# Moving two blocks of work in a routed-attention and feed-forward kernel: pair 0's sums and clusters past the first weight chunk, the last pair's denominators up to its products with v

## The chip, the cores and the metric

The kernel runs on one core of a Trainium2 chip. The metric is the device time of one execution in microseconds (us), lower is better. All times "at 18.26" are counted from the start of the span of the profiled execution. The engines are TensorE (PE in the profile; PEld is its weight load), VectorE (DVE), ScalarE (ACT), GpSimd (POOL) and SyncE (SP), which issues most of the DMA transfers. Each engine works through its own instructions in order; an instruction that waits holds up what stands behind it on the same engine.

## The reference

Four batches, eight heads, 768 tokens, 64 values per head, 16 clusters per head. A query sees only the keys of its own cluster. The result, with the heads side by side, goes through a normalisation and a two-layer feed-forward block (512 to 2048 to 512).

```python
q_n = q / (norm(q) + 1e-6); k_n = ...; c_n = ...
q_assign = argmax(q_n @ c_n.T, axis=-1)
k_assign = argmax(k_n @ c_n.T, axis=-1)
mask = q_assign[:, None] == k_assign[None, :]
scores = where(mask, q @ k.T / sqrt(D), -1e9)
attn = exp(scores - max) ; attn = attn / (sum(attn) + 1e-9)
x = attn @ v                      # heads side by side: (4, 768, 512)
xn = (x - mean) / sqrt(var + 1e-6) * g_ln
out = x + maximum(xn @ w_ch1, 0) @ w_ch2
```

The two weight matrices come as 64-bit floats; the kernel turns them into 32-bit floats itself.

## The kernel before, in words

**Attention.** Two heads of a batch make a pair; there are 16 pairs, n = 0 to 15. Each pair has two slots, one for each half of the queries (384), and each slot has six steps, one for each tile of 128 keys. Per step, `scores` multiplies the mask's one-hot rows (a large negative number is added where the clusters differ), then k and q (L385), into a PSUM tile `s_ps`, of which there are three, and ScalarE takes the exponential into `e` (L380). `weigh` multiplies six steps' `e` with v (L397) into `a_ps`, which ScalarE copies to `x` (L412). `add_up` adds the slot's `e` tiles on VectorE (`two`, L432 and L435; for the last pair `es`, L422, five additions).

**Clusters.** For the next pair, VectorE transposes k and q (L282), TensorE multiplies them with the normalised centroids (`sim_ps`, L304), and `prep_route` finds the best cluster on VectorE: transpose, maximum, comparison, transpose (L317, L320, L323, L333), which leaves `oh`. ScalarE makes the mask's rows out of `oh` in `prep_mask` (L350), six pieces in the slot before the pair starts.

**Denominators.** `finish(n, 0)` sums the added-up exponentials over the keys with a matmul by ones (`den_ps`, L451), copies the result on ScalarE (L460), and sends it through DRAM with two POOL transfers (`flat`, `rdens`). `finish(n, 1)` takes the reciprocal on VectorE (L467) and spreads it; parts 2 and 3 multiply `x` by it and store it. For n < 15 `den_ps` is in the pool of `a_ps`; for n = 15 it is a tile of the pool that `ps()` names at that moment.

**Weight chunks.** The weights come in 32 chunks of 512 KB. SP loads a chunk into `raw` (two buffers, L241). `split_weight` takes the words apart on VectorE (L250, L253, L256), `join_weight` builds the 32-bit value from them (L265, L269, L270) and sends the low part as a POOL transfer that adds into `w` (L273). `convert` gives chunk m a place: chunks 0 to 13 go with both slots of pairs 0 to 6, chunks 14 to 21 with the first slot of pairs 7 to 14, the last ten follow in the feed-forward part. `load_weight(m + 2)` stands behind `join_weight(m)`.

**Order.** In the attention part the order of TensorE, VectorE, ScalarE and POOL is the order of the calls in the loop over `u` (pair and slot); SP's transfers are placed by the framework's scheduler there, in an order near to that of the calls. In each slot: scores; the similarities or the masks of the next pair; `split_weight`; `weigh`; `add_up`; `join_weight`; in slot 0 the load of the next pair's v and `prep_route(n + 1)`.

**Hand-over.** After the last pair all pools of the attention part, PSUM's three among them, are closed (`stage.close()`), and a pool of eight PSUM tiles, `ps_m`, takes their place. The feed-forward part begins with the products `x_ps`, `y_ps`, `z_ps` (`first_layer`, L781), copies on ScalarE (`p`, `u`, L796) and additions on VectorE (L801). The last pair's `finish(15, 0)` stands between the second and the third of these products, so its `den_ps` is a tile of `ps_m`. The first blocks of the feed-forward part read batch 0, whose attention is long done.

Of the kernel before, what the change touches and what calls it, by code (L numbers as in the profile page):

```python
# [19 lines left out]
def kernel(  # L20
# [49 lines left out]
    def ps(name, dt=F32, n=512):  # L70
        return pools["t"].tile([P, n], dt, tag="t", name=name)

    pairs = [(b, pr) for b in range(B) for pr in range(NPAIR)]
# [170 lines left out]
    def split_weight(m):  # L244
        words = raws[m].bitcast(U32).rearrange("p (n w) -> p n w", w=2)
        hi = words[:, :, 1]
        ta = pools["conv"].tile([P, WC], U32, tag="ta", name="ta")
        tb = pools["conv"].tile([P, WC], U32, tag="tb", name="tb", bufs=2)

        nc.vector.tensor_scalar(  # L250
            ta, hi, 0x07FFFFFF, 3, op0=ALU.bitwise_and, op1=ALU.logical_shift_left
        )
        nc.vector.scalar_tensor_tensor(  # L253
            out=ta, in0=hi, scalar=0xC0000000, in1=ta, op0=ALU.bitwise_and, op1=ALU.bitwise_or
        )
        nc.vector.tensor_single_scalar(tb, hi, 0x7FF00000, op=ALU.bitwise_and)  # L256
        halves[m] = (ta, tb)
# [56 lines left out]
    def prep_route(n):  # L314

        sim = route.tile([P, HC], F32, tag="sim", name="sim_sb")
        nc.vector.transpose(sim, prepared[n]["sim"][:, :HC])  # L317
        sims = sim.rearrange("p (g c) -> p g c", c=NCL)
        best = route.tile([P, NG], F32, tag="best", name="best")
        nc.vector.tensor_reduce(best, sims, AX.X, ALU.max)  # L320

        onehot = route.tile([P, HC], BF16, tag="onehot", name="onehot")
        nc.vector.scalar_tensor_tensor(  # L323
            out=onehot.rearrange("p (g c) -> p g c", c=NCL),
            in0=sims,
            scalar=1.0,
            in1=best.unsqueeze(2).to_broadcast([P, NG, NCL]),
            op0=ALU.mult,
            op1=ALU.is_equal,
            accum_out=hits[:, n : n + 1],  # L330
        )
        oh = route.tile([P, HC], BF16, tag="oh", name="oh")
        nc.vector.transpose(oh, onehot)  # L333
        prepared[n]["oh"] = oh
# [107 lines left out]
    def finish(n, part):  # L442
        b, pr = pairs[n]
        if part == 0:
            den = ps_a.tile([P, 512], F32, tag="a", name="den_ps") if n + 1 < len(pairs) else ps("den_ps")
            parts = len(sums[n, 0])
            for h in range(parts):
                for j in range(2):
                    for g in range(NHALF):
                        r = (j * NHALF + g) * Q  # L450
                        nc.tensor.matmul(  # L451
                            den[r : r + Q, :HC], ones, sums[n, g][h][:, j, :],
                            start=h == 0, stop=h == parts - 1, tile_position=(0, r),
                            skip_group_check=True,
                        )
            if n + 1 < len(pairs):
                dsb = last.tile([P, HC], F32, tag="dsb", name="dsb", bufs=1)
            else:
                dsb = late["all"][:, 1, :HC]
            nc.scalar.copy(dsb, den[:, :HC])  # L460
            flat = dram.tile([P // Q, HC], F32, tag="flat", name="flat")
            nc.gpsimd.dma_start(out=flat, in_=dsb[0:P:Q, :])
            nc.gpsimd.dma_start(
                out=rdens[:, n, :], in_=flat.rearrange("i (p e) -> (i p) e", e=DE)
            )
        elif part == 1:
            nc.vector.reciprocal(rdens[:, n, :], rdens[:, n, :])  # L467
            row = dram.tile([2, S], F32, tag="row", name="row")
            nc.gpsimd.dma_start(
                out=row.rearrange("j (p e) -> (j p) e", e=DE), in_=rdens[:, n, :]  # L470
            )
            if n + 1 < len(pairs):
                rb = last.tile([P, S], F32, tag="rb", name="rb", bufs=1)
            else:
                rb = late["all"][:, 2]
            for j in range(2):
                nc.gpsimd.dma_start(
                    out=rb[j * D : (j + 1) * D, :],
                    in_=row[j : j + 1, :].to_broadcast([D, S]),
                )  # L480
            late[n] = rb
        elif part == 2:
            a, x = xs.pop(n), late[n]
            if b:
                nc.vector.tensor_tensor(x, a, x, ALU.mult)
                nc.sync.dma_start(out=xT_d[b][pr], in_=x)
            else:
                late[n] = norm_tiles(b)[0][:, pr, :]
                nc.vector.tensor_tensor(late[n], a, x, ALU.mult)
        else:  # L490
            x = late.pop(n)

            if n + 1 < len(pairs):
                y = last.tile([P, S], F32, tag="y", name="y")
            else:
                y = late["all"][:, 0]
            nc.vector.transpose(y, x)
            for i in range(P // Q):
                m = pr * P + i * Q
                nc.sync.dma_start(  # L500
                    out=x_d[b].rearrange("t (a r) m -> r (t a) m", r=Q)[:, :, m : m + Q],
                    in_=y[i * Q : (i + 1) * Q].rearrange("r (g f) -> r g f", f=Q),
                )
# [182 lines left out]
    with tc.manual_schedule(engines=order | {mybir.EngineType.Pool}):  # L686
        for u in range(len(pairs) * slots):
            n, slot = divmod(u, slots)
            nxt = n + 1 < len(pairs)
            own = range(GROUP * u, GROUP * (u + 1))  # L690
            if slot == 0 and not nxt:
                finish(n - 1, 0)
            if slot == 0 and nxt:
                for side in (1, 0):
                    prep_transpose(n + 1, side)
                    load(n + 2, "qk"[side])
            for i in own:
                if i >= AHEAD:
                    scores(i)
            if slot == 0:  # L700
                if n and nxt:
                    finish(n - 1, 0)
                if n:
                    prep_mask(n, *pieces[-1])
                if nxt:
                    prep_sims(n + 1)
            elif nxt:
                for piece in pieces[:-1]:
                    prep_mask(n + 1, *piece)
            for job in extra.pop((n, f"between {slot}"), ()):  # L710
                job()
            if slot and n > 1 and nxt:
                finish(n - 2, 2)
                finish(n - 2, 3)
            m = convert.get((n, slot))
            if m is not None:
                split_weight(m)
            for i in own:
                weigh(i)
            add_up(n, slot, (0,))  # L720
            if slot and n and nxt:
                finish(n - 1, 1)
            if nxt:
                add_up(n, slot, (1,))
            if m is not None:
                join_weight(m)
                load_weight(m + 2)
            if slot == 0:
                load(n + 1, "v")
                if nxt:  # L730
                    prep_route(n + 1)
                else:
                    for part in (2, 3):
                        finish(n - 2, part)
                    finish(n - 1, 1)
            elif not nxt:
                for part in (2, 3):
                    finish(n - 1, part)
            for job in extra.pop((n, slot), ()):
                job()  # L740

# [203 lines left out]
    with tc.manual_schedule(engines=order):  # L945
        first_layer(0, 0, 1)
        first_layer(0, 0, 2)
        finish(len(pairs) - 1, 0)
        first_layer(0, 0, 6)
        w1_sums(0, 0, (2, 3))  # L950
        x_sum(0, 3)
        first_layer(0, 0, 5)
        first_layer(0, 0, 7)
        x_sum(0, 4)
        w1_sums(0, 1)
        for j in range(1, NFH):
            first_units(0, j)
            if j in (1, 3):
                for part in ((1,), (2, 3))[j // 2]:
                    finish(len(pairs) - 1, part)  # L960
# [252 lines left out]
```

## Time and profile before

| | |
|---|---|
| median of 5 runs | 919.44 us (918.18, 919.24, 919.44, 920.58, 921.9) |
| profiled execution | 917.51 us, span 915.5 us |
| granted TensorE clock | 0.998 |
| TensorE matmuls | 905.1 us busy, 99% of the span |
| VectorE | 605.8 us, 66% |
| ScalarE | 365.3 us, 40% |
| GpSimd | 78.1 us, 9% |
| DMA | 89.33 MB, mean 98 GB/s |

The page gives each engine's busy time, then forty slices of the span with the busy share in tenths. Rows of groups and of the timeline name the source line, the engine, the operation and the tiles it writes and reads (`e<-s_ps`); `[0.61 <-DVE oh L333]` behind a row of the timeline says that the engine stood idle for 0.61 us before it and that VectorE's `oh` ended the wait. In the table of waits the columns are total, times and the longest. Attention lasts from about 9 to 329 us, the feed-forward part from there to the end. From 20 to 310 us VectorE is busy about nine tenths of the time as well.

### The profile page before, as it was taken

The page shows a single profiled execution, that of the slowest core. Times are in us where ns is not written, and L with a number is a line of the kernel's source. Part 1 is how long each engine was busy: PE and PEld are TensorE (multiplying, and loading weights), DVE is VectorE, ACT ScalarE, POOL GpSimd, SP SyncE. Part 2 cuts the span into 40 slices and gives each one's busy share as a digit, 9 for nine tenths or more (in the row PEclk, how much of TensorE's full clock was granted, in tenths as well). Part 3 has the DMA queues.
Part 4 walks back from the last instruction along what each step waited for, and adds up shares of the span by engine and source line. Part 5 has one row for each costly group of instructions (what it writes and reads, how often), then busy time and mean ns, then how long its engine had stood idle before and what let it go on. Part 6 is the DMA issues. An engine that isn't in the chain of part 4 may idle for free.

```text
span 915.5 us, 12230 instructions
## 1 busy us (share of the span) xinstructions
PE 905.1 (99%) x4556; PEld 577.1 (63%) x4556; DVE 605.8 (66%) x1060; ACT 365.3 (40%) x619; POOL 78.1 (9%) x141
## 2 busy tenths in 40 slices
PE   8999999999999999999999999999999999999997
PEld 5444444444444455578885568886558887557886
DVE  6999999999889878988943446552436372445331
ACT  4777777998877643330003330003331001332000
POOL 1122322121121112100000000000000000000000
PEclk9999999999999999999999999999999999999999
DMA  7898999998986246663420003120002120000011
GB/s 154 145 192 165 185 178 196 189 204 162 204 172 124 69 129 155 139 170 114 167 79 0 1 0 104 54 73 11 1 1 92 47 76 29 0 1 12 24 47 38
DMA packets 186579, 89.33 MB, mean 98 GB/s; under 512 B 153632, under 2 KB 170128, under 8 KB 186512
## 3 DMA queue, kind: packets, MB, share of 16 engines
q1 hardware_dynamic: 177200, 73.09, 34.1%
q0 software_dynamic: 7712, 14.99, 8.4%
q8 instruction: 38, 0.62, 0.3%
q10 hardware_dynamic: 1600, 0.39, 0.2%
q14 instruction: 29, 0.24, 0.1%
HBM read 62.52 MB, written 17.52 MB: 87 GB/s over the span
## 4 chain that ended last, share of the span: by engine, by line
PE 65%; ACT 0%; DVE 0%; issue 0%
PE x_ps L874 18%; PE x_ps L781 18%; PE z_ps L874 9%; PE z_ps L781 9%; PE y_ps L874 5%; PE y_ps L781 5%; PE s_ps L385 1%; PE a_ps L397 1%; PE den_ps L451 0%; ACT late L412 0%; DVE o_sb L897 0%; PE stat_ps L564 0%; PE flag_ps L756 0%
## 5 line engine op out<-in xcount | busy, mean ns | idle before, releaser
L380 ACT ACTIVATE e<-s_ps 128x768 f32<-128x768 f32 x192 | 151.3, 813 | 9.2 <-PE s_ps L385 5.0
L385 PE MATMUL s_ps<-t,t 64*128 64x384 f32 x768 | 155.0, 483 | 0.0
L397 PE MATMUL a_ps<-e,v_sb 128*64 128x384 f32 x768 | 130.9, 490 | 0.0
L397 PEld LDWEIGHTS a_ps<-e,v_sb 128*64 128x64 f32 x768 | 52.3, 137 | 75.8 <-issue 63.0
L801 DVE TENSOR_TENSOR h<-z_ps,u 128x384 f32<-128x384 f32 x64 | 35.6, 556 | 89.8 <-PE z_ps L781 67.4
L385 PEld LDWEIGHTS s_ps<-t,t 64*128 64x128 f32 x768 | 68.3, 188 | 34.4 <-issue 33.5
L874 PE MATMUL x_ps<-w2t,h 128*128 128x256 f32 x384 | 84.5, 379 | 0.0
L809 ACT ACTIVATE h<-h 128x384 f32<-128x384 f32 x96 | 49.5, 522 | 86.4 <-DVE h L801 86.3
L874 PEld LDWEIGHTS x_ps<-w2t,h 128*128 128x128 f32 x384 | 72.7, 190 | 10.1
L385 PE MATMUL s_ps<-mask,mask 64*128 64x384 bf16 x384 | 63.2, 324 | 1.1 <-ACT e L380 0.7
L432 DVE TENSOR_TENSOR two<-e 128x1536 f32<-128x1536 f32 x30 | 52.6, 1754 | 12.2 <-ACT e L380 11.9
L796 ACT COPY u<-x_ps 128x384 f32<-128x384 f32 x64 | 30.6, 479 | 74.8 <-PE x_ps L781 74.8
L796 ACT COPY p<-x_ps 128x384 f32<-128x384 f32 x32 | 15.0, 467 | 97.6 <-PE x_ps L781 97.6
L435 DVE TENSOR_TENSOR two<-two,e 128x1536 f32<-128x1536 f32 x30 | 52.7, 1756 | 1.7
L885 DVE TENSOR_TENSOR o_sb<-x_ps,xb 128x256 f32<-128x256 f32 x48 | 20.2, 420 | 49.5 <-PE x_ps L874 49.5
L781 PE MATMUL x_ps<-xn,w 128*128 128x384 f32 x128 | 46.6, 487 | 0.6 <-ACT late L412 0.6
L781 PE MATMUL x_ps<-xt,ws 128*128 128x384 f32 x128 | 46.6, 487 | 0.0
L781 PE MATMUL y_ps<-xn,w 128*128 128x384 f32 x128 | 46.5, 486 | 0.0
L781 PE MATMUL z_ps<-xt,ws 128*128 128x384 f32 x128 | 46.5, 486 | 0.0
L781 PE MATMUL x_ps<-xn,ws 128*128 128x384 f32 x128 | 46.5, 486 | 0.0
L781 PE MATMUL x_ps<-xt,w 128*128 128x384 f32 x128 | 46.5, 486 | 0.0
L781 PE MATMUL z_ps<-xn,ws 128*128 128x384 f32 x128 | 46.5, 486 | 0.0
(151 smaller groups left out, 1331.8 us busy)
## 6 DMA issues: line engine op xcount, KB each, us to landing
raw<-in_moe_w_ch_dram SPq DMA_DIRECT2D x32, 512.0 KB, 5.2
w<-tb POOLq DMA_DIRECT2D x32, 256.0 KB, 6.3
v_sb<-in_v_dram SPq DMA_DIRECT2D x32, 192.0 KB, 5.5
xr<-x_d SPq DMA_DIRECT2D x24, 256.0 KB, 3.2
xb<-x_d SPq DMA_DIRECT2D x48, 128.0 KB, 2.2
out_dram<-o_sb SPq DMA_DIRECT2D x48, 128.0 KB, 1.7
q_sb<-in_q_dram SPq DMA_DIRECT2D x62, 96.0 KB, 3.5
k_sb<-in_k_dram SPq DMA_DIRECT2D x62, 96.0 KB, 5.6
```

The costliest lines, as they stand in the source:

```text
L380: nc.scalar.activation(e, s[:, :, :HC], AF.Exp, scale=SCALE)
L385: nc.tensor.matmul(s[:, j, :HC], of_keys[:, keys], of_queries[:, o : o + HC], start=part == first, stop=part != first, skip_group_check=True,)
L397: nc.tensor.matmul(acc[j * D : (j + 1) * D, :HC], loaded[n]["v"][:, j, c, :], e[:, j, :], start=(c == 0), stop=(c == NT - 1),)
L432: nc.vector.tensor_tensor(two, soft.pop(u), soft.pop(u + 1), ALU.add)
L435: nc.vector.tensor_tensor(two, two, soft.pop(u + 2), ALU.add)
L781: nc.tensor.matmul(bank[:, :HC], lhs[:, c, :], rhs[:, c, :], start=first and c == 0, stop=c == NDH - 1, skip_group_check=True,)
L796: nc.scalar.copy(t, bank[:, :HC])
L801: nc.vector.tensor_tensor(h, bank[:, :HC], other, ALU.add)
L809: nc.scalar.activation(h, h, AF.Relu)
L874: nc.tensor.matmul(bank[:, :MH], hidden[lhs + (c,)][:, tt * P : (tt + 1) * P], rhs[:, c, :], start=first and c == 0, stop=c == NFH - 1, sk ...
L885: nc.vector.tensor_tensor(o, bank[:, :MH], x, ALU.add)
```

## The change

Two blocks of calls are moved; no instruction is added or removed.

- In slot 0 of pair 0, `split_weight(0)` and `join_weight(0)` (and `load_weight(2)`) no longer stand around `weigh` and `add_up`. They follow `prep_route(1)`. So on VectorE the order is now: the two sums of slot 0, the four operations of pair 1's clusters, then the six operations of chunk 0. On SP the two loads of pair 1's v now go ahead of chunk 2's load.
- `finish(15, 0)` is called at the end of the last slot, directly behind the last products with v and while the attention part's pools are still open. On TensorE `den_ps` now stands ahead of the first `x_ps`, and on ScalarE its copy ahead of the first `p`. It takes its tile from the one-tile pool `ps_t` instead of `ps_m`. The order of POOL's instructions stays.

```diff
             m = convert.get((n, slot))
-            if m is not None:
+
+            if m:
                 split_weight(m)
             for i in own:
                 weigh(i)
...
             if nxt:
                 add_up(n, slot, (1,))
-            if m is not None:
+            if m:
                 join_weight(m)
                 load_weight(m + 2)
             if slot == 0:
                 load(n + 1, "v")
                 if nxt:
                     prep_route(n + 1)
+                    if m == 0:
+                        split_weight(m)
+                        join_weight(m)
+                        load_weight(m + 2)
                 else:
...
             elif not nxt:
                 for part in (2, 3):
                     finish(n - 1, part)
+                finish(n, 0)
...
         first_layer(0, 0, 1)
         first_layer(0, 0, 2)
-        finish(len(pairs) - 1, 0)
         first_layer(0, 0, 6)
```

## The prediction

> **What bounds the kernel now.** I read the page's first two parts, then TensorE's waits over the whole span, then the timeline around the two places that the change touches. The first part and two rows of slices:
>
> ```profile
> PE 905.1 (99%) x4556; PEld 577.1 (63%) x4556; DVE 605.8 (66%) x1060; ACT 365.3 (40%) x619; POOL 78.1 (9%) x141
> ...
> PE   8999999999999999999999999999999999999997
> ...
> PEclk9999999999999999999999999999999999999999
> ```
>
> TensorE is busy in every slice at full granted clock. A change can shorten the run only by taking idle time from TensorE. Its waits are few:
>
> ```profile
> PE den_ps L451 <- ACT x L412: 1.2, 1, 1.2
> ...
> PE s_ps L385 <- ACT e L380: 0.7, 2, 0.6
> PE x_ps L781 <- ACT late L412: 0.6, 1, 0.6
> PE s_ps L385 <- ACT mask L350: 0.4, 1, 0.4
> ```
>
> Columns: total, times, longest, in us. They sum to 2.9 us; the largest (at 309.8, pair 14) is not touched by the change. Busy time can hide gaps, because the ends of matmuls are modelled. So I also took the start of each block of matmuls from the timeline: scores of six steps take 4.95 us from their start to the next block's, products with v 4.02, sums of two tiles 1.31, similarities 0.78. These hold in every pair to 0.02, with three exceptions after 16.9 us: the scores that begin at 29.88 (5.10), those at 219.54 (5.30, statistics follow), and the products at 304.57 (5.25, the 1.2 above). The Trainium skill, Perfetto Trace Analysis, section Identifying the Most-Contended Engine, says that matmul busy time does not tell the distance to TensorE's peak; by LDWEIGHTS' 63% a third would be free. That is headroom for other matmuls; a reordering gains idle time alone, and by the steady block times there is almost none.
>
> **Part one: pair 0's sums and pair 1's clusters ahead of the first weight chunk.** The rows of VectorE and ScalarE:
>
> ```profile
> 18.26 0.43 DVE L250 TENSOR_SCALAR ta<-raw 128x512 uint32<-128x512 uint32 x1 [2.21 <-DMA raw<-in_moe_w_ch_dram]
> 19.67 1.75 DVE L432 TENSOR_TENSOR two<-e 128x1536 f32<-128x1536 f32 x1
> ...
> 24.98 0.58 DVE L317 STREAM_TRANSPOSE sim_sb<-sim_ps 128x384 f32<-128x384 f32 x1
> ...
> 27.40 0.61 ACT L350 ACTIVATE mask<-oh,of_head 128x384 bf16<-128x384 bf16 x1 [0.61 <-DVE oh L333]
> ...
> 31.59 4.33 ACT L380 ACTIVATE e<-s_ps 128x768 f32<-128x768 f32 x6
> ```
>
> VectorE stands 2.21 us idle for the first raw chunk; behind that stand the sums, the rest of the chunk and the clusters of pair 1 (L317 to L333, 24.98 to 27.37). ScalarE's masks wait 0.61 for the result. They end at 31.19, so the copy of x and the first exponential come late, and TensorE's fourth pair of score tiles, which needs the first exponential's buffer, starts at 32.45, where its step of 0.81 would give 32.34. With 0.03 at the second tile this is the 5.10 against 4.95.
>
> After the change: the transposes end at 16.06 as before. The two sums need the six exponentials, done by 16.63, so they run from 16.1 to 19.7 (1.75 + 1.76 and starts). The clusters take 2.39 us, to 22.1. The chunk's first three operations (1.49 by their row: 18.26 to 19.75) and its last three (1.87: 23.20 to 25.07) go to 25.5; the chunk landed at 18.26 and its wait is gone. The second chunk's split starts at 25.5 instead of 27.29. What is late next: the masks, which now stand behind the exponentials that end at 26.79, so they start at 26.8 instead of 27.40 and end 0.6 earlier; the first exponential starts at about 31.0 and TensorE's fourth tile no longer waits. That is **0.14 us** off the path. The remaining 1.8 us of VectorE's lead buy nothing: clusters of pair 3 and later are ready 3.1 to 4.9 us ahead of ScalarE's masks, those of pair 2 2.0 us ahead.
>
> Queues: on SP the two loads of v for pair 1 pass ahead of the third chunk. They wait for no VectorE work, so they go out after q's last load, at about 23.6 instead of 25.47. The third chunk waits for the first one's last read, at 25.5 instead of 25.10. Its use is at 35.77 in this trace (without a wait), about 34 with VectorE's lead; a chunk here took 5.8 us from issue to landing, so it lands at about 31.3. The Trainium skill, DMA: Bandwidth & Descriptors, section Two DMAs through the same engine are not ordered, says that descriptors of one queue of a DMA engine start in order; by that v's 0.39 MB now stand ahead of the chunk, 2.4 us more at the 163 GB/s of this stretch, and the chunk would land at 33.7: still in time. POOL's addition of the first chunk moves from 25.38 to about 25.8, and nothing but the far layer reads it. Bounds for part one: -0.15 (all of the 5.10 against 4.95) to +0.15 (the same loss once more at pair 2, if its 2.0 us are used up). I take -0.14.
>
> **Part two: the last pair's denominators.** The chain of what ended last:
>
> ```profile
> 324.59 4.05 PE a_ps L397 x24
> ...
> 328.66 0.49 ACT late L412
> ...
> 329.19 1.56 PE x_ps L781 x4
> 330.75 1.29 PE y_ps L781 x4
> 332.04 0.78 PE den_ps L451 x8
> 332.82 1.49 PE x_ps L781 x4
> ```
>
> The products with v end at 328.61; x_ps waits 0.58 for ScalarE's copy of their result; the denominators come 2.8 us later. The change puts them at 328.6. Their input, the last sum es, ends at 328.22, so no wait is added, but 0.3 us is all that is left of a margin of 3.75 (331.97 less 328.22). They take 0.78, and would cover the 0.58. But the product's wait moves too: it waits for whoever last reads the closed pools' PSUM. In the built program of before its count is that of the copy of a_ps, in the changed one it is one higher, the copy of den_ps, now the last reader. That copy started 0.92 after den_ps's first matmul (332.89 less 331.97) and takes 0.48: from 328.54 it ends at 329.94, and x_ps starts at 329.99 instead of 329.19. That is 0.80 lost, and 0.78 won where den_ps stood: **+0.02 us**. Behind it, x_ps's second product waits for the copy p, which ends at 332.1 against a need at 332.8; its third waits for VectorE's xn (333.29 to 334.24, now 0.8 later, 335.04) against 335.46. Both are covered. POOL's flat and rdens transfers go out 3.4 us earlier, but their reader (L467, 347.00) keeps its place on VectorE. Bounds: -0.58 if the wait is covered after all, +0.58 if it becomes as long as the 1.16 of the den_ps at 309.82, TensorE's longest behind a ScalarE copy. I take +0.02, the nearest row.
>
> **Sum.** -0.14 + 0.02 = -0.12 us. The profiled execution took 917.51 us (span 915.5, 2.0 around it), so 917.39; the median of the runs is 919.44, 1.93 above it, which I carry over: **919.3 us**. The costs' ends together are -0.73 to +0.73.
>
> **Rivals.** *The first chunk lands later in ordinary executions (faster).* The profile shows one landing, and it had no reserve: every microsecond that it comes after 18.26 delays VectorE, then the masks, then TensorE. Afterwards it may come 3.8 us later (22.1) at no cost. For it: the runs lie 0.7 to 4.4 us above the profiled one, unexplained. Against it: every load of the first 16 us can vary as well, and those stay exposed. If all 1.93 of the median's surplus were this wait, the time would be 919.44 - 1.93 - 0.12 = 917.4.
>
> *The denominators meet a late es (slower).* TensorE works in order, and all of the feed-forward stands behind den_ps. If VectorE ends es later by d, TensorE loses d - 0.3; before, 3.75 us covered it. The longest wait of VectorE for an exponential in this same pair was 2.9 (es at 313.29); met here it costs 2.6, and with the 0.12 the time is 921.9. It decides from d = 0.3 and is measurable from d = 2.3. Against it: VectorE reached this es with no idle time, from 318 on, so exponentials do not set it.
>
> *The product waits for its own bank alone (the wait is covered).* -0.14 - 0.56 = -0.7: 918.7. The count in the program speaks against it.
>
> **How the numbers follow.** About 0.2% (1.84 us) is what a measurement of this kernel can tell from no change. The forecast 0.70; chunk late 0.14; es late 0.08; wait covered 0.08. Of the chunk's case I count 0.10 over the bound, of es's 0.05; scatter of the medians adds 0.02 on each side. So faster 0.12, slower 0.07, within 0.2% 0.81. Range: the costs' ends (918.7 to 920.2) widened by 1.1, the larger distance from the median to a neighbour among the middle three runs: 917.6 to 921.3, and down to 917.4 for the late chunk.
>
> **What would show it.** Right: no VectorE wait for raw near 18, oh ready by about 22, scores of pair 1 in 4.95; den_ps at 328.5 less 0.14 and a TensorE idle of about 0.6 ahead of x_ps, released by the copy of den_ps. Wrong: an idle of TensorE ahead of den_ps, x_ps without a wait, a new VectorE wait for the third chunk, or block times that differ elsewhere.

## The result, and the profile after

| | before | after |
|---|---|---|
| median | 918.22 us (91 runs, 916.65 to 922.58) | 916.85 us (46 runs, 915.59 to 918.22) |
| lower and upper quartile | 917.68, 919.22 | 916.69, 917.38 |
| runs over 919 us | 28 of 91 | 0 of 46 |
| profiled execution | 917.51 us, span 915.5 | 917.44 us, span 915.4 |

The ratio is 0.9982, 95% interval 0.9977 to 0.9987: faster by 0.18%, which is 1.65 us by the ratio (the two medians lie 1.37 apart). The two profiled executions differ by 0.1 us of span. So a single profile shows next to none of the gain; it sits in the scatter of the runs, and mostly in its upper half (1.0 us between the lower quartiles, 1.8 between the upper ones).

TensorE's waits in the profile after (total, times, longest, in us):

```profile
PE den_ps L451 <- ACT x L412: 1.2, 1, 1.2
...
PE x_ps L787 <- ACT late L460: 0.6, 1, 0.6
...
PE s_ps L385 <- ACT mask L350: 0.4, 1, 0.4
```

The wait ahead of `x_ps` is as long as before, but it is now ended by the copy of the denominators (L460) instead of the copy of `a_ps` (L412). VectorE and ScalarE in pairs 0 and 1, from the timeline after:

```profile
19.62 0.58 DVE L317 STREAM_TRANSPOSE sim_sb<-sim_ps 128x384 f32<-128x384 f32 x1
...
21.93 0.39 DVE L250 TENSOR_SCALAR ta<-raw 128x512 uint32<-128x512 uint32 x1
...
26.97 0.61 ACT L350 ACTIVATE mask<-oh,of_head 128x384 bf16<-128x384 bf16 x1
```

No brackets stand behind these rows: VectorE waits for no chunk, the clusters start at 19.62 instead of 24.98, and ScalarE's masks no longer wait for `oh`. TensorE's scores of pair 1, first from the timeline of before, then from that after, each with the first row of the block and the first row behind it:

```profile
29.88 0.40 PE L385 MATMUL s_ps<-mask,mask 64*128 64x384 bf16 x2
...
34.98 1.50 PE L451 MATMUL den_ps<-two,ones 128*32 128x384 f32 x16
```

```profile
30.04 0.34 PE L385 MATMUL s_ps<-mask,mask 64*128 64x384 bf16 x2
...
34.99 1.50 PE L451 MATMUL den_ps<-two,ones 128*32 128x384 f32 x16
```

That is 5.10 us before and the steady 4.95 after; the block starts 0.15 later after, because pair 0's products do (17.04 against 16.89), which offsets the gain in the span. The hand-over, from the timeline of TensorE and ScalarE:

```profile
328.52 0.85 PE L451 MATMUL den_ps<-es,ones 128*32 128x384 f32 x8
...
329.44 0.48 ACT L460 COPY late<-den_ps 128x384 f32<-128x384 f32 x1 [0.33 <-PE den_ps L451]
329.97 1.56 PE L787 MATMUL x_ps<-xn,w 128*128 128x384 f32 x4 [0.60 <-ACT late L460]
...
335.24 1.46 PE L787 MATMUL x_ps<-xn,ws 128*128 128x384 f32 x4
```

The denominators start without a wait, and `x_ps` waits 0.60 behind them.

### The profile page after: what moved, and what is told of

The parts are those of the page before. It is cut to its first block, busy times and chain, and to the rows that moved or that the text cites. A ratio compares the mean times of both kernels' runs of the same rounds, so it can differ in the third digit from the quotient of the medians.

```text
span 915.4 us, 12228 instructions
## 1 busy us (share of the span) xinstructions
PE 905.1 (99%) x4556; PEld 577.9 (63%) x4556; DVE 605.4 (66%) x1060; ACT 365.1 (40%) x619; POOL 78.2 (9%) x141
## 4 chain that ended last, share of the span: by engine, by line
PE 65%; ACT 0%; DVE 0%; issue 0%
PE x_ps L880 18%; PE x_ps L787 18%; PE z_ps L880 9%; PE z_ps L787 9%; PE y_ps L880 5%; PE y_ps L787 5%; PE s_ps L385 1%; PE a_ps L397 1%; PE den_ps L451 0%; ACT late L460 0%; DVE o_sb L903 0%; PE stat_ps L564 0%; PE flag_ps L762 0%
## 5 line engine op out<-in xcount | busy, mean ns | idle before, releaser
L397 PE MATMUL a_ps<-e,v_sb 128*64 128x384 f32 x768 | 130.9, 490 | 0.0
L397 PEld LDWEIGHTS a_ps<-e,v_sb 128*64 128x64 f32 x768 | 52.3, 137 | 75.8 <-issue 62.8
```

Of the source, the lines that this page charges most:

```text
L397: nc.tensor.matmul(acc[j * D : (j + 1) * D, :HC], loaded[n]["v"][:, j, c, :], e[:, j, :], start=(c == 0), stop=(c == NT - 1),)
```

## The experiments

Theories: **the late chunk** (the first weight chunk often lands later than in the profile of before; before, TensorE paid for that, now it doesn't), **part two** (the gain is at the hand-over), and **small steps** of both. A fourth came from the change's side effect: v's loads of pair 1 pass ahead of chunk 2 on SP. All ratios are to the kernel before, run on the same chip beside the experiment.

**Part one alone.** The diff of the change without its two lines on `finish`.

> Only part one of the change: pair 0's sums and pair 1's clusters ahead of the first weight chunk; the last pair's denominators stay where they were. Theory (the first chunk lands later in ordinary executions than in the profiled one, and every microsecond of that reached TensorE before): nearly the whole gain of the change, 1.2 to 1.6 us below the kernel before, with a much narrower scatter. Rival one (the gain is part two's, at the hand-over): 0.1 to 0.2 us. Rival two (both parts by small steps): about half, 0.7 us.

Measured: median 916.76 against 918.02, ratio 0.9984 (0.9975 to 0.9994); 0 of 12 runs over 919, of the kernel before 6 of 35. Its scatter is that of the whole change, and the scores of pair 1 take 4.95 in its profile.

**Part two alone.**

```diff
                 for part in (2, 3):
                     finish(n - 1, part)
+                finish(n, 0)
...
         first_layer(0, 0, 2)
-        finish(len(pairs) - 1, 0)
```

> Only part two: the last pair's denominators directly behind its products with v. Theory of the late chunk: 0.1 to 0.2 us below the kernel before (by the two profiles, den_ps starts 0.02 earlier and the third x_ps product 0.20 earlier), and the wide scatter of the kernel before stays. Rival one (the gain is part two's): 1.2 to 1.6 us. Rival two: 0.7 us.

Measured: ratio 0.9999 (0.9986 to 1.0011); 4 of 12 runs over 919. The wide scatter stays. So the gain is part one's, and part two's 0.1 to 0.2 us is within what the times leave open. The traces show it: from the start of the last products with v to TensorE's last matmul, the five profiles with part two take 585.23 us each and the nine without it 585.40, so part two is worth 0.17 us.

**The first two chunks' loads exchanged, before and after the change.** The same edit in both kernels:

```diff
-        load_weight(0)
-        load_weight(1)
+        load_weight(1)
+        load_weight(0)
```

> The kernel before with the loads of the first two weight chunks exchanged, so that chunk 0 lands one chunk later, by an estimate 2.2 us (512 KB at the 231 GB/s that the profile of before shows from 16.9 to 20.9). Theory of the late chunk: VectorE's wait at 18 grows from 2.2 to about 4.4 us, pair 1's clusters, ScalarE's masks and TensorE's scores at 29.88 come as much later, and the run is 1.5 to 2.2 us slower than the kernel before. Rivals: VectorE has room for it, no more than 0.3 us.

> The changed kernel with the same exchange of the first two chunks' loads. Theory of the late chunk: the chunk is not needed before 21.9, so nothing is lost: the time of the changed kernel, 1.2 to 1.7 us below the kernel before, and no wait of VectorE for raw above 0.3 us. If it is slower than the changed kernel by over 0.5 us, the order has less reserve than the profile shows.

Measured: the late kernel before 1.0024 (1.0010 to 1.0038), median 920.92; the late changed kernel 0.9980 (0.9970 to 0.9989), median 916.14, both against 918.02. A later chunk costs the one 2.2 us by the ratio (2.9 by the medians) and the other nothing. The chunk came later than I had worked out, 3.6 us instead of 2.2, and the profile of the late kernel before shows two separate ways to TensorE, and a loss of clock behind them. VectorE and ScalarE, from its timeline:

```profile
21.81 0.43 DVE L250 TENSOR_SCALAR ta<-raw 128x512 uint32<-128x512 uint32 x1 [5.76 <-DMA raw<-in_moe_w_ch_dram]
...
25.06 2.92 ACT L380 ACTIVATE e<-s_ps 128x768 f32<-128x768 f32 x4 [1.51 <-DVE two L432]
30.95 0.61 ACT L350 ACTIVATE mask<-oh,of_head 128x384 bf16<-128x384 bf16 x1 [2.97 <-DVE oh L333]
```

and TensorE:

```profile
25.93 0.34 PE L385 MATMUL s_ps<-mask,mask 64*128 64x384 bf16 x2 [0.81 <-ACT e L380]
...
32.24 0.33 PE L385 MATMUL s_ps<-mask,mask 64*128 64x384 bf16 x1 [1.32 <-ACT mask L350]
33.52 0.48 PE L385 MATMUL s_ps<-mask,mask 64*128 64x384 bf16 x1 [0.94 <-ACT mask L350]
...
34.96 0.63 PE L385 MATMUL s_ps<-mask,mask 64*128 64x384 bf16 x2
35.28 1.47 PE L385 MATMUL s_ps<-t,t 64*128 64x384 f32 x4
```

First the sums: VectorE adds pair 0's exponentials late, their four buffers `e` stay occupied, ScalarE's exponentials stand 1.51 and TensorE's sixth score tile 0.81. Then the clusters: the masks wait 2.97, and TensorE twice more behind them. By its block starts TensorE lost 5.1 us against the steady times here, 1.0 of it through the buffers. Not all of it is waiting: from 33.1 to 36.5 the granted clock was 0.5, against 1.0 on both sides. The last two rows show it (0.63 and 1.47 us, where the same groups take 0.33 and 0.81 at full clock). From the second mask matmul at 33.52 to the denominators at 39.92 TensorE took 6.4 us; in the first repeat below, behind the same wait of 0.94 but at full clock, it took 5.0 (31.46 to 36.48). By this estimate about 1.4 of the 5.1 us are clock and about 2.7 the waits for the masks. My prediction had only the second way, and no price for the clock.

The mean granted clock of ordinary runs fits this. In 8 of the 12 runs of this kernel it is 0.997, and these took 920.79 us or more. Of the 85 runs of the kernel before beside the experiments, six show 0.996 or 0.997, all at 920.89 or more. No run of a kernel with the sums or the clusters ahead of the chunk is below 0.998. That the waits bring the lower clock on is inferred from this and from one trace. How long a wait has to be is not shown: the 1.16 us at pair 14 left the clock at 1.0 in every profile that has it.

**The sums alone ahead of the chunk; the clusters stay behind it.** SP's order is then that of before.

```diff
-            if m is not None:
+            if m:
                 split_weight(m)
...
+            if m == 0:
+                split_weight(m)
             if m is not None:
                 join_weight(m)
```

> The kernel before with only pair 0's two sums moved ahead of chunk 0's split; join and then pair 1's clusters stay behind the chunk, and SP's loads stay in the order of before. Theory of the late chunk: from the profile of before, the sums end at 19.7, the chunk is needed from then on (1.5 us of reserve against 18.3), and the clusters end at about 25.5, 1.3 us ahead of ScalarE: most of part one's gain, 1.0 to 1.4 us below the kernel before. Rival (part one's gain comes from v's loads passing ahead of chunk 2 on SP): none of it, within 0.2 us of the kernel before.

Measured: median 916.74 against 917.87, ratio 0.9989 (0.9977 to 1.0000); 0 of 11 runs over 919, of the kernel before 9 of 33. The interval ends at 1.0000, so by the ratio alone the gain is at the edge of what can be told; the scatter says more: with the next experiment 0 of 22 runs are over 919. The gain does not need v's loads ahead of chunk 2. In its profile VectorE comes to the chunk at 19.48 and does not wait.

> The same with the loads of the first two chunks exchanged, so that chunk 0 lands at about 21.8 as in the late kernel before. Sums early, clusters late: no wait of ScalarE's exponentials for VectorE's sums near 25, but the clusters end at about 27.5 to 28 and the masks wait 0.7 to 1.2 us. Theory: 2.5 to 4 us below the late kernel before, 0 to 0.6 us over the kernel before's undisturbed time near 917. If only the sums' buffers had mattered, it would be as fast as the changed kernel (916.8); if only the clusters, as slow as the late kernel before (920.9) less what their earlier end saves.

Measured: 916.69, ratio 0.9990 (0.9979 to 1.0001), 0 of 11 runs over 919. My forecast missed because the chunk did not come at 21.8 in the profile. VectorE and ScalarE, from its timeline:

```profile
20.26 0.43 DVE L250 TENSOR_SCALAR ta<-raw 128x512 uint32<-128x512 uint32 x1 [1.06 <-DMA raw<-in_moe_w_ch_dram]
...
26.47 0.61 ACT L350 ACTIVATE mask<-oh,of_head 128x384 bf16<-128x384 bf16 x1
```

VectorE waits 1.06 here, and the masks do not wait: `oh` is written from 25.38 and ScalarE is free at 26.4. The sums alone give enough cover for a chunk at 20.3. What happens at 21.8 was not seen.

**The clusters alone ahead, the sums behind the split, loads exchanged.**

```diff
+            if m == 0:
+                prep_route(n + 1)
             if m is not None:
                 split_weight(m)
...
                 if nxt:
-                    prep_route(n + 1)
+                    if m != 0:
+                        prep_route(n + 1)
```

> The kernel before with pair 1's clusters moved ahead of chunk 0's split, the two sums still between its split and its join, and the first two chunks' loads exchanged. Clusters early, sums late: no wait of the masks for oh, but ScalarE's exponentials of slot 1 wait about 1.5 us for the sums' buffers and TensorE's sixth score tile 0.8 to 1.0 us, as in the late kernel before. Expected: 0.9 to 1.1 us over the changed kernel, near 917.8. If the buffers cost nothing, 916.8.

In the profile the way through the buffers stands alone. VectorE and ScalarE, from its timeline:

```profile
21.62 0.43 DVE L250 TENSOR_SCALAR ta<-raw 128x512 uint32<-128x512 uint32 x1 [2.17 <-DMA raw<-in_moe_w_ch_dram]
...
24.87 2.92 ACT L380 ACTIVATE e<-s_ps 128x768 f32<-128x768 f32 x4 [1.34 <-DVE two L432]
```

TensorE's scores of that slot take 5.76 instead of 4.95: 0.81 us, a little less than expected, and the scores of pair 1 are steady. This execution took 917.98, near the forecast of 917.8, but the median is 916.49 (ratio 0.9988, 0.9977 to 0.9999): six of the 11 runs lie between 916.26 and 916.49, three between 917.81 and 918.16. The trace gives the mechanism, the times leave open how often ordinary executions pay its price.

**Pair 14's denominators in another PSUM tile**, on top of the change, for the largest wait that is left:

```diff
-            den = ps_a.tile([P, 512], F32, tag="a", name="den_ps") if n + 1 < len(pairs) else ps("den_ps")
+            den = ps_a.tile([P, 512], F32, tag="a", name="den_ps") if n + 2 < len(pairs) else ps("den_ps")
```

> The changed kernel, and pair 14's denominators take their tile from the one-tile pool that the last pair's take, instead of the pool of a_ps, so that they need not wait for ScalarE's copy of x (1.16 us idle of TensorE at 309.8, the largest of the run). If that wait just goes: 1.1 us below the changed kernel, near 915.7, and no idle at 309. If another wait takes its place (the scores' masks, or the first exponential behind ScalarE's copies): less, down to nothing.

Measured: median 915.57 against 917.87, ratio 0.9970 (0.9957 to 0.9984), span 913.5 in the profile. TensorE's timeline at pair 14 has no idle time left:

```profile
304.04 4.09 PE L397 MATMUL a_ps<-e,v_sb 128*64 128x384 f32 x24
308.06 0.85 PE L451 MATMUL den_ps<-two,ones 128*32 128x384 f32 x8
308.85 0.34 PE L385 MATMUL s_ps<-mask,mask 64*128 64x384 bf16 x2
```

The products take 4.02 to the next block instead of 5.25, and no other wait took its place. It is the fastest version, though its interval still touches that of the change.

**Three more profiled executions of the kernel before**, unchanged, called first, second and third repeat below.

> The kernel before, unchanged: another profiled execution. Theory of the late chunk: its time above 917 is the lateness of chunk 0. VectorE's wait for raw ends later than 18.3 by about as much as the scores and products of pairs 0 and 1 exceed their steady block times, and that excess less the 0.15 us of the first profile is its span over 915.5, to some 0.5 us. If a slow execution shows no such excess, most of the scatter comes from elsewhere.

> The same kernel once more, the same expectation: span over 915.5 equals the excess of TensorE's blocks from 20 to 36 us, with VectorE's wait for raw as late.

> The same kernel a third time, the same expectation. Three looks at a kernel whose runs are over 919.5 in about one case of four may all be fast ones; then they say only how far the landing of the chunk varies.

The first repeat caught a late chunk (919.50 us, span 917.7). VectorE's rows of its timeline:

```profile
19.75 0.43 DVE L250 TENSOR_SCALAR ta<-raw 128x512 uint32<-128x512 uint32 x1 [3.44 <-DMA raw<-in_moe_w_ch_dram]
...
28.28 0.58 DVE L333 STREAM_TRANSPOSE oh<-onehot 128x384 bf16<-128x384 bf16 x1
```

ScalarE's and TensorE's rows behind them, from the same timeline:

```profile
28.90 0.61 ACT L350 ACTIVATE mask<-oh,of_head 128x384 bf16<-128x384 bf16 x1 [1.85 <-DVE oh L333]
...
30.19 0.33 PE L385 MATMUL s_ps<-mask,mask 64*128 64x384 bf16 x1
31.46 0.32 PE L385 MATMUL s_ps<-mask,mask 64*128 64x384 bf16 x1 [0.94 <-ACT mask L350]
```

The whole start of an execution also shifts, so the landing must be read against something. I take the start of pair 0's products (the first row of L397) and set beside it by how much the time from there to the end of pair 1's scores exceeds the steady 17.94 (twice 4.02 and 4.95). Five profiled executions have part one's code of before:

| execution | products start | chunk's split starts | between | over the steady 17.94 |
|---|---|---|---|---|
| second repeat | 17.84 | 19.09 | 1.25 | 0.03 |
| profile of before | 16.89 | 18.26 | 1.37 | 0.15 |
| part two alone | 16.27 | 17.94 | 1.67 | 0.44 |
| third repeat | 16.79 | 18.58 | 1.79 | 0.58 |
| first repeat | 17.15 | 19.75 | 2.60 | 1.39 |

In these five, from 1.22 on, every microsecond of lateness is a microsecond of TensorE, to 0.01. In the late kernel before the split starts 4.93 behind the products (21.81 less 16.88); the same line gives 3.7 there and the trace shows 5.1; the difference is the 1.4 put down to the clock above. In all seven profiles with the sums ahead of the chunk the scores of pair 1 take 4.95. With the change the chunk is wanted 4.89 after the products' start (21.93 less 17.04). The spans follow only in part: the first repeat is 2.2 over 915.5, of which 1.2 is this excess over the first profile's, 0.6 a wait at pair 8 (below), 0.3 a later start and 0.1 the stretch behind TensorE's last matmul. That stretch varies as well, from 4.9 to 6.1 us in the fourteen profiles. The second repeat is 0.5 over with next to no excess: its products start 0.95 later, and its last stretch is 0.4 shorter. That expectation failed: the chunk is one source of the scatter and not the only one.

**The exchange together with the PSUM tile.**

> The changed kernel with pair 14's denominators in the other PSUM tile and the loads of the first two chunks exchanged. The exchange alone gave 916.14 against 916.85 for the changed kernel, inside the scatter. If it is worth something by itself, 915.0 or less; if not, the 915.6 of the kernel without the exchange, within 0.3 us.

Measured: 916.25, ratio 0.9972 (0.9959 to 0.9985), against 0.9970 without the exchange. One of its 12 runs took 920.02 us, at a mean clock of 1.0, and is not explained. A gain of the exchange by itself, which the 916.14 above had suggested, is not confirmed.

## Why the prediction was wrong

The sign was right, the size was not: 0.12 us forecast, 1.65 measured, and the median of 916.85 lies under the range's 917.4.

**Part one, the step that failed.** "I take -0.14", with bounds of -0.15 to +0.15, was worked out from one landing of the chunk. For that execution it is right: the profile after has 4.95 where before had 5.10. But the prediction itself held that the landing "had no reserve", and a wait that ends a chain without reserve has to be priced by its scatter, not by one draw. The table shows 0.03 to 1.39 us for the same code. The sum should have gone by the rival of the late chunk, which I gave 0.14 and priced at up to 2.05 us; the 1.65 lie under that price. That the price came so near is partly luck: it was the whole surplus of a median of five runs, which stood 1.2 us above that of 91. The hint stood in the first table: the profiled execution was the fastest of the six known.

**The ways into the wait.** I named the clusters and the masks. The runs showed a second way, the buffers of the exponentials that wait for the sums: 0.8 to 1.0 us in two profiles with the chunk at 21.6 and 21.8. The sums ahead of the chunk are therefore worth moving on their own, and alone they gave 0.9989 (0.9977 to 1.0000). A third term was missing: the lower clock behind a long wait, about 1.4 us in the one trace that has it.

**The reserve.** That the chunk may come 3.8 us later at no cost was right in kind: with the loads exchanged the changed kernel lost nothing and the kernel before lost 2.2 us.

**SP's order.** Right: the third chunk landed in time (its first use is at 33.74, without a wait), VectorE waits for no chunk in pairs 1 to 3, and the sums alone, with SP's order unchanged, had no run over 919 either.

**Part two.** Right in mechanism: the wait moved behind the denominators with 0.60 instead of 0.58, because `x_ps` waits for the last reader of the closed pools, and `es` was in time. The term was +0.02; by the trace it is -0.18 (from 328.54 to 328.52 at the start, 335.44 to 335.24 at the third `x_ps` product). From the last products with v to the first `x_ps` the loss is the 0.02 forecast. The 0.2 won comes from the blocks that stood beside `den_ps`, which the sum put at nothing: `y_ps` took 1.38 to the next block and the product behind `den_ps` 1.40, where 1.29 is steady and both take 1.29 after. The first `x_ps` product takes 1.40 in both kernels. The timed ratio of part two alone, 0.9999, neither confirms nor excludes 0.18 us.

**The base.** 919.44 was the median of five runs, 91 gave 918.22. With -0.12 on it the forecast would have been 918.1. So 1.2 of the 2.45 us by which I missed came from the base. The rest came from the change: 0.2 by part two's traces, and part one for what is left. The base itself moves between groups of runs: beside the experiments the kernel before had medians of 918.02, 917.87 and 919.12.

**Rivals on the slower side.** Not seen: no wait ahead of `den_ps`; the covered wait of `x_ps` was not seen either.

**What stays open.** The excess in the five profiled executions is 0.5 us on the mean; with part two's 0.17 that is still less than half of the 1.65 that the runs show. That ordinary executions see the chunk later than these five would fit, and so would the lower clock of the highest runs, but none of them has a trace of this kind. Shown is that part one carries the gain, that a later chunk slows the one kernel and not the other, and that the excess follows the lateness; the share of each in the 1.65 is not.

## What to carry to other kernels

Where the profile shows an engine waiting for a transfer, and the chain behind that wait reaches the bounding engine without reserve, one profiled execution gives one draw of its cost, and a long wait can cost more than its length if the clock drops behind it: compare the profiled time with the other runs, look at several executions, and put work that does not need the transfer ahead of it. In this kernel TensorE's wait at the closing of the PSUM pools went to whoever read them last, so moving a matmul into the gap moves the wait behind it. A one-buffer PSUM tile shared by two users can cost more than a reordering gains: naming another free tile for pair 14's denominators took 1.2 us of idle time out of TensorE.

## What the runs showed of the hardware

The first use of a transfer at the start of an execution varies by more than a microsecond for the same code: chunk 0's split started at 17.94 to 19.75, and 1.25 to 2.60 us behind the start of the same products, in five executions. Part of this is the issue: SP issued the load at 12.13 to 13.07, and the split started 5.72 to 6.68 behind that. With the two 512 KB loads exchanged it was 20.26, 21.62 and 21.81 in three profiles that show VectorE waiting for it, against 18.26 before: 2.0 to 3.6 us, not the 2.2 worked out from the traffic.

The granted clock of TensorE was 0.5 for 3.4 us behind waits of 1.32 and 0.94 us that followed each other with one matmul between them (the late kernel before). It stayed at 1.0 behind the wait of 0.94 us in the first repeat and behind those of 1.16 us at pair 14.

There is a second wait of this kind that the change does not touch. In nine of the fourteen profiles ScalarE waits 0.2 to 2.0 us for the rows of the normalisation in pair 8. From ScalarE's timeline of the first repeat:

```profile
162.89 0.63 ACT L535 ACTIVATE xr<-xr 128x512 f32<-128x512 f32 x1 [1.60 <-DMA xr<-x_d]
```

TensorE's scores from 162.84 on take 5.51 there instead of 4.95, and 5.71 at 161.47 in the changed kernel with the loads exchanged, where ScalarE waits 2.00. Waits of up to 1.15 there cost TensorE nothing; the profile of before has none, the profile after one of 0.74.
